# A transformer block with local attention, forward and backward: normalisation in one step, one set of stores on another queue, and a later set of shift copies

## The chip, the core and the metric

The kernel runs on one core of a Trainium2 chip. The core has five engines with instruction streams of their own: TensorE (PE in the profile; PEld is its loading of weights), VectorE (DVE), ScalarE (ACT), GpSimd (POOL) and SyncE (SP). SP computes nothing and issues transfers; ACT and POOL issue transfers as well, between their own instructions. A transfer that an engine issues stands in that engine's instruction stream: it is issued when everything ahead of it in the stream has been and when what it waits for is done. In the profile, SPq, ACTq and POOLq are these issues. The transfers themselves are carried by 16 DMA engines.

The metric is the device time of one execution in microseconds (us), as a median over several executions.

## What is computed

One pre-norm transformer block on x of 2048 rows (S) and 512 columns (D), and the gradients of all its inputs for a given gradient of the output. Everything is bf16.

```python
def _layernorm(x, axis=-1, eps=1e-5):
    m = jnp.mean(x, axis=axis, keepdims=True)
    v = jnp.var(x, axis=axis, keepdims=True)
    return (x - m) / jnp.sqrt(v + eps)

# attention: 32 heads of 16 columns, 8 keys per row at distances 0, 2, ..., 14
idx = pos[:, None] - off[None, :]
logits = jnp.einsum("bhsd,bhswd->bhsw", q, kg) * scale
attn = _softmax(logits, axis=-1)
o = jnp.einsum("bhsw,bhswd->bhsd", attn, vg)

h = x + _A_ref(_layernorm(x, axis=-1), A_wqkv, A_wo)
h2 = h + _B_ref(_layernorm(h, axis=-1), B_w1, B_b1, B_w2, B_b2)   # GELU network, F = 1792

_out, _vjp = jax.vjp(_f, A_x, A_wqkv, A_wo, B_w1, B_b1, B_w2, B_b2)
_grads = _vjp(grad_out)
```

The layernorm has no learned scale or offset. It is applied twice: to x and to h.

## The kernel before

The 2048 rows are worked through in four chunks (NC = 4) of 512 rows (CH), each as four tiles (TPC = 4) of 128 rows, one row per partition. The program has three phases.

Phase 1 (0 to about 185 us) is the forward attention: for each chunk the first layernorm, the projection to q, k and v, the logits, the softmax, the weighted sum over the eight keys, the output projection, h, and the second layernorm. Here a scheduler at build time places the instructions of each engine, by estimated costs, from the program's dependencies. So an edit of one instruction can move others.

Phase 2 (185 to about 380 us) is the GELU network forward and backward, chunk by chunk (p2_h, p2_rest), almost only matmuls. At its end p3_pre works out the gradient of the attention output for chunk 0.

Phase 3 (380 us to the end) is the backward pass of the attention. Its order is written out by hand. The loop `for c in range(NC + 2)` runs over the chunks; within it `slot(us)` is a place where DVE is expected to be busy for so long and PE is filled with other work, which `wgrads` gives out: the matmuls of the weight gradients (ps_gw for the network's weights, ps_gwo and ps_gwq for the attention's). `later(n, cost, fn)` puts a small piece of work (some transposes and a copy, for instance) off by n slots. There is no scheduler behind it: what is called first stands first on its engine.

The pieces that the change touches:

**layernorm (L165 to L180).** For each of the four tiles of a chunk, statistics on DVE: st (L169), then mean and variance into mv (L170), whose last index 0 is the mean and 1 the variance. Then for the four tiles at once: ve, the variance plus epsilon (L173, DVE); rstd, that to the power −1/2 (L174, POOL); nm, which is −mean × rstd (L176, DVE). At last ln for each tile (L178, DVE), x × rstd + nm, with rstd and nm as scalars of each partition. It is called for x (four chunks, ending in ln1) and for h (four chunks, ending in ln2): eight calls, 32 ln instructions. Transposes on PE (pt, L162) read ln.

**to_tm_store (L204 to L219).** It brings a feature-major tile to rows: eight transposes on PE (ptm, L210), one ACT copy of 128x1024 (tmst, L213), one store of 256 KB (L215). It does so twice for a chunk. A further store of 18 KB (L217 or L219) puts the 18 border rows into the neighbour chunk's table. All stores are issued by SP. In phase 1 it writes v_d, k_d and q_d. With `stage` given it is called in p3_pre (L681, chunk 0) and in p3_go (L1054, chunks 1 to 3), and writes go_d, the gradient of the attention output: eight stores of 256 KB and three of 18 KB. POOL then gathers rows of go_d into R (L224). In phase 3 tmst has two buffers.

**What else SP issues in phase 3.** Loads for the weight gradients: gwm (L753, 1 MB, in turn into two buffers, so that a load waits for the matmuls that read the buffer before), ln_r (L741, 1 MB), gqh (L855), and ln1r (L151), vw (L885). ln1r is the chunk's normalised x.

**What ACT does in phase 3.** got (L647, L653), ghT (L163), gqkvT (L280), gqs and gks (L1029), the shift copies sh (L1062), gyr (L184), and gwst (L831): the copy of a finished weight-gradient accumulator (ps_gw, ps_gwo or ps_gwq, pool psF with two buffers) from PSUM, and every second time ACT issues its store. PE can open an accumulator only when gwst has emptied the buffer.

**The products.** R, the rows gathered by POOL, is multiplied on DVE by coefficients cf (prb, L1012; in phase 1 L262). PE sums the products (ps_band, L1026), and ACT copies the sum out.

**shift (L1058 to L1066).** It copies the logit gradients glf (or attn), moved along the rows by 4 × w4, into sh: four ACT copies of 32x1024, one for each quarter of the partitions (about 1 us each). Its `at` gives the number of slots by which each copy is put off. Then `coefs` transposes sh into cf on DVE. For the last chunk (c == NC) the call is

```python
        if c == NC:
            shk = shift(c - 1, glf, (1, 1, 2, 2))
```

and its cf are used by the key part (cfk) four tiles later in that pass; the value part (vtile) is worked on meanwhile.

Of the kernel before, what the change touches and what calls it, by code (L numbers as in the profile page):

```python
# [10 lines left out]
P = 128  # L11
BF16 = mybir.dt.bfloat16
F32 = mybir.dt.float32
ACT = mybir.ActivationFunctionType
ALU = mybir.AluOpType
# [16 lines left out]
def _sub(apobj, dims, off=0):  # L32
    return _ap(apobj, [apobj.ap[0]] + [list(d) for d in dims], off)
# [3 lines left out]
def kernel(  # L37
# [21 lines left out]
    V, A, T, G, SY = nc.vector, nc.scalar, nc.tensor, nc.gpsimd, nc.sync  # L59
# [7 lines left out]
    CH = 512  # L67
    NC = S // CH
    TPC = CH // P
# [33 lines left out]
    def TT(name):  # L103
        return psT.tile([P, 1024], BF16, name=name, tag="t")
# [24 lines left out]
    RPAD = 18  # L129
# [35 lines left out]
    def layernorm(wp, src, rstd_all, c, dst):  # L165
        mv = wp.tile([P, TPC, 2], F32, name="mv", tag="mv", bufs=2)
        for j in range(TPC):
            st = wp.tile([P, 6], F32, name="st6", tag="st6", bufs=2)
            V.bn_stats(out=st[:], in_=src[:, j, :])  # L169
            V.bn_aggr(out=mv[:, j, :], in_=st[:])  # L170
        rs = rstd_all[:, c * TPC:(c + 1) * TPC]
        ve = wp.tile([P, TPC], F32, name="ve", tag="ve", bufs=2)
        V.tensor_scalar(out=ve[:], in0=mv[:, :, 1], scalar1=EPS, scalar2=None, op0=ALU.add)  # L173
        G.tensor_tensor(out=rs, in0=ve[:], in1=mhalf[:], op=ALU.pow)  # L174
        nm = wp.tile([P, TPC], F32, name="nm", tag="nm", bufs=2)
        V.scalar_tensor_tensor(out=nm[:], in0=mv[:, :, 0], scalar=-1.0, in1=rs, op0=ALU.mult, op1=ALU.mult)  # L176
        for j in range(TPC):
            V.tensor_scalar(out=dst[:, j, :], in0=src[:, j, :], scalar1=rs[:, j:j + 1], scalar2=nm[:, j:j + 1],  # L178
                            op0=ALU.mult, op1=ALU.add)

    def ln_bwd_a(wp, ps, rs):
        gyr = wp.tile([P, D], BF16, name="gyr", tag="gyr", bufs=2)
# [19 lines left out]
        ln_bwd_v(wp, gyr, c0, xh, resid, out)  # L202

    def to_tm_store(wp, fm, off, dst, c, back, nb=3, stage=None):  # L204
        for j2 in range(TPC // 2):
            pt = TT("ptm")
            for jj in range(2):
                j = 2 * j2 + jj
                for g in range(4):
                    T.transpose(_sub(pt[:], [[32, DH], [1, 8]], jj * 512 + 8 * g),  # L210
                                fm[:, g, off + j * P:off + (j + 1) * P], Pmat[:])
            st = stage() if stage else wp.tile([P, 2, 512], BF16, name="tmst", tag="tmst", bufs=nb)
            A.copy(out=st[:], in_=pt[:].rearrange("p (a n) -> p a n", a=2))  # L213
            r = j2 * 2 * P + (RPAD if back else 0)
            SY.dma_start(out=dst[c][r:r + 2 * P, :].rearrange("(a p) d -> p a d", p=P), in_=st[:])  # L215
            if back and j2 == 1 and c + 1 < NC:
                SY.dma_start(out=dst[c + 1][0:RPAD, :], in_=st[P - RPAD:P, 1, :])  # L217
            if not back and j2 == 0 and c > 0:
                SY.dma_start(out=dst[c - 1][CH:CH + RPAD, :], in_=st[0:RPAD, 0, :])  # L219

    def gather_rows(R, dst, c, sc, back):
        t = dst[c]
# [303 lines left out]
    glf = glp.tile([P, 2, SP], BF16, name="glf")  # L526
# [128 lines left out]
    def ga_prod(pr, got, vw, g):  # L655
        V.tensor_tensor(out=pr, in0=got[:, g, :].unsqueeze(1).to_broadcast([P, W, 512]),  # L656
                        in1=_sub(vw[:, g, PAD:PAD + 512], [[-DIL, W], [1, 512]]), op=ALU.mult)

    def ga_sum(L, pr, g):
        for hf in range(2):  # L660
            for w4 in range(4):
                T.matmul(L[32 * w4:32 * w4 + 32, hf, :], lhsT=Emat[:, g, :], rhs=pr(2 * w4 + hf),
                         start=(g == 0), stop=(g == 3), skip_group_check=True)
# [141 lines left out]
    def pt3(tag, name=None):  # L805
        if tag in HOME:
            shp, *hs = HOME[tag]
            pl, tg = hs[hpos[tag] % len(hs)]
            hpos[tag] += 1
            return pl.tile(shp, BF16, name=name or tag, tag=tg, bufs=1)  # L810
        shp, nb = P3T[tag]
        return p3.tile(shp, BF16, name=name or tag, tag=tag, bufs=nb)
# [155 lines left out]
    def later(n, cost, fn):  # L968
        pend.append([n, cost, fn])

    def slot(dve_us):
        pe = 0.0
        for x in list(pend):
            x[0] -= 1
            if x[0] <= 0:
                pend.remove(x)
                x[2]()
                pe += x[1]
        filler(dve_us * RATIO - pe)
# [78 lines left out]
    def shift(c, src, at):  # L1058
        sh = pt3("sh")

        def cp(w4):
            A.copy(out=sh[32 * w4:32 * w4 + 32],  # L1062
                   in_=_sub(src[32 * w4:32 * w4 + 32, 0, 0:1], [[SP + 2, 2], [1, 512]], c * CH + 4 * w4))
        for w4 in range(4):
            later(at[w4], 0.0, lambda w4=w4: cp(w4))
        return sh  # L1066
# [33 lines left out]
    for c in range(NC + 2):  # L1100
        if 0 < c < NC:
            got, vw = st3[c]["got"], st3[c]["vw"]
            L = psL.tile([P, 2, 512], F32, name="ps_ga", tag="l")
            for g in range(4):
                pr = pt3("prod", "pr")
                ga_prod(pr[:], got, vw, g)
                later(2, 0.7, lambda pr=pr, g=g, L=L: ga_sum(L, lambda w: pr[:, w, :], g))
                if c >= 2:
                    gln1(c - 2, g)
                slot(2.3 + (1.9 if c >= 2 else 0))  # L1110
            if c + 1 < NC:
                load_vw(c + 1)
        elif c >= NC:
            for g in range(4):
                gln1(c - 2, g)
                slot(2.0)
            if c == NC + 1:
                for _ in range(3):
                    slot(2.0)
                break  # L1120
        if c > 0:
            gt_ = pt3("gqkvT")
            gqkv[c - 1] = gt_
            for sc in range(2):
                later(1 + sc, 1.0, lambda sc=sc, c=c, gt_=gt_: unperm(gqs[c - 1][sc][:], gt_[:, 0:4, :], 4, sc * 256))
            cfv = coefs(pt3, st3[c - 1]["sh"][:, 0, 0:1], 0, 512)

        def vtile(k):
            sc, m = k // 2, k % 2
            if m == 0:  # L1130
                bt["gs"] = pt3("gks")
            gs = bt["gs"]
            band_tile("v", c - 1, sc, m, cfv, gs, 1.0,
                      lambda gs=gs, sc=sc, c=c: unperm(gs[:], gqkv[c - 1][:, 8:12, :], 4, sc * 256))

        if c == NC:
            shk = shift(c - 1, glf, (1, 1, 2, 2))
        if c > 0:
            vtile(0)
            vtile(1)  # L1140
        if 0 < c < NC:
            pp = pt3("pp")
            V.tensor_tensor(out=pp[:], in0=L[:], in1=attn_c(c), op=ALU.mult)
            later(1, 0.9, lambda L=L, pp=pp: ga_rows(L, pp))
        if c > 0:
            vtile(2)
            vtile(3)
        if 0 < c < NC:
            V.tensor_tensor(out=glf[:, :, c * CH:(c + 1) * CH], in0=L[:], in1=attn_c(c), op=ALU.mult)
            if c == 1:  # L1150
                V.memset(glf[:, :, S:SP], 0.0)
        if c < NC:
            cfq = coefs(pt3, glf[:, 0, 0:1], c * CH, SP)
        if 0 < c < NC:
            shk = shift(c - 1, glf, (1, 2, 3, 3))
        if c == NC:
            later(2, 0.0, lambda: open_gates.add("v"))
        if 0 < c < NC - 1:
            p3_go(c + 1)
        if c < NC:  # L1160
            st3[c]["sh"] = shift(c, attn, (4, 5, 6, 7) if c > 0 else (2, 3, 4, 5))
            gqs[c] = []
            for k in range(4):
                sc, m = k // 2, k % 2
                if m == 0:
                    gqs[c].append(pt3("gqs"))
                band_tile("q", c, sc, m, cfq, gqs[c][sc], scale, None)
            if c == NC - 1:
                later(3, 0.0, lambda: open_gates.add("q"))
        if c > 0:  # L1170
            cfk = coefs(pt3, shk[:, 0, 0:1], 0, 512)
            for k in range(4):
                sc, m = k // 2, k % 2
                if m == 0:
                    bt["gs"] = pt3("gks")
                gs = bt["gs"]
                band_tile("k", c - 1, sc, m, cfk, gs, scale,
                          lambda gs=gs, sc=sc, c=c: unperm(gs[:], gqkv[c - 1][:, 4:8, :], 4, sc * 256))
            if c == NC:
                slot(0.5)  # L1180
                slot(0.5)
                slot(0.5)
                open_gates.add("k")
# [53 lines left out]
```

## Time and profile before

| | us |
|---|---|
| median of 4 executions | 663.56 |
| the four | 665.61, 661.72, 660.21, 665.4 |
| the profiled execution | 670.66 |
| its span (first to last instruction) | 668.5 |

The page of the profile gives busy time by engine, the span in 40 slices and the chain of work that ended last. Two lines of the slices:

```profile
PEclk9899999898889999999999999999999999999999
DMA  9483848744999996997995999886798679997621
```

Each digit is a slice of 16.7 us. PEclk is the TensorE clock granted, in tenths of full speed (9 is 90% or more); DMA is the mean busy share of the 16 DMA engines. Two lines of the waits of SP's queue tell what its stream stood still for: in total, how often, and the longest time.

```profile
SPq L215 <- ACT tmst L213: 162.7, 26, 24.0
SPq L753 <- PE ps_gw L896: 51.9, 6, 14.3
```

In an engine's timeline a line has the start, the duration, the engine, the code line, the operation with its tiles and shapes, the number of instructions, and in brackets the idle time before it with what ended it. In a chain a line has start, duration and the work, in order of time.

### The profile page before, as it was taken

Reading aid. Unit: us, or ns where it says so; the run is one execution under the profiler, and the core shown is the slowest. Engines: PE = TensorE matmul, PEld = TensorE weight load, DVE = VectorE, ACT = ScalarE, POOL = GpSimd, SP = SyncE. Lnnn points to the kernel's source line nnn. Section 1 sums busy time; section 2 is a strip of 40 time slices with the busy share of each in tenths; the row PEclk is TensorE's granted clock in tenths of the full one; section 3 lists DMA queues with packets and bytes.
Section 4 is the critical chain, followed back from the end, with each engine's and each line's share of the span. In section 5 each row is a group of like instructions: output and inputs, shape, how many; then the busy total and the mean of one; then the engine's idle time right before and its main releaser. Section 6 shows DMA issues by size and latency. Waiting matters only on the chain.

```text
span 668.5 us, 10227 instructions
## 1 busy us (share of the span) xinstructions
PE 600.9 (90%) x3916; PEld 289.7 (43%) x3916; DVE 517.7 (77%) x760; ACT 375.7 (56%) x601; POOL 150.0 (22%) x183
## 2 busy tenths in 40 slices
PE   3889989696699989999999979989999999979897
PEld 1343444342344434444444433434466667434343
DVE  7889979878889768888849769867877789569230
ACT  2497878688585457377351353673368337455321
POOL 3341536431101110110110222221232023112010
PEclk9899999898889999999999999999999999999999
DMA  9483848744999996997995999886798679997621
GB/s 288 158 268 127 293 154 293 237 144 94 225 245 208 233 248 139 248 235 159 258 289 156 277 333 370 305 292 249 236 392 288 255 232 332 363 306 254 206 79 47
DMA packets 147947, 158.98 MB, mean 238 GB/s; under 512 B 94476, under 2 KB 132540, under 8 KB 141244
## 3 DMA queue, kind: packets, MB, share of 16 engines
q1 hardware_dynamic: 120076, 69.58, 41.1%
q0 software_dynamic: 15376, 77.63, 33.5%
q10 hardware_dynamic: 12448, 11.14, 5.2%
q8 instruction: 30, 0.49, 0.3%
q14 instruction: 17, 0.14, 0.1%
HBM read 87.76 MB, written 48.03 MB: 203 GB/s over the span
## 4 chain that ended last, share of the span: by engine, by line
PE 59%; ACT 11%; DMA 9%; DVE 6%; issue 5%; POOL 2%; SPq 0%; ACTq 0%; DVEq 0%; POOLq 0%
PE ps_gg L622 7%; PE ps_gl L1082 6%; PE ps_gl L636 6%; PE ps_gwq L924 6%; PE ps_gw L904 6%; PE ps_gw L896 5%; PE ps_h L577 4%; PE ps_f L610 4%; DMA gwm<-gT_d 3%; PE ps_band L1026 2%; PE ps_gwo L914 2%; PE ptu L279 2%; DMA R<-k_d,rowi 2%; DMA goT<-in_grad_out_dram 2%; ACT sh L1062 1%
## 5 line engine op out<-in xcount | busy, mean ns | idle before, releaser
L1012 DVE TENSOR_TENSOR prb<-R,cf 128x2048 bf16<-128x2048 bf16 x96 | 111.5, 1219 | 29.8 <-PE ps_band L1026 22.8
L184 ACT ACTIVATE gyr<-ps_gl,rstd 128x512 bf16<-128x512 f32 x32 | 22.0, 687 | 86.1 <-PE ps_gl L636 48.8
L577 PE MATMUL ps_h<-ln2T,w 128*128 128x512 bf16 x224 | 58.3, 390 | 4.4 <-ACT xa L579 4.0
L896 PE MATMUL ps_gw<-gout_r,gwm 128*128 128x512 bf16 x224 | 53.1, 384 | 3.3 <-DMA gwm<-gT_d 3.3
L622 PE MATMUL ps_gg<-goT,w2T 128*128 128x512 bf16 x224 | 54.5, 379 | 0.9 <-DVE gb1p L624 0.8
L610 PE MATMUL ps_f<-w,gt 128*128 128x512 bf16 x224 | 51.3, 379 | 3.9 <-ACT h2s L613 2.0
L904 PE MATMUL ps_gw<-gwm,ln_r 128*128 128x256 bf16 x448 | 52.9, 273 | 0.7 <-ACT gwst L831 0.7
L636 PE MATMUL ps_gl<-w1T,dt 128*128 128x512 bf16 x224 | 52.0, 379 | 0.6 <-ACT gyr L184 0.4
L924 PE MATMUL ps_gwq<-gqh,ln_r 128*128 128x512 bf16 x192 | 44.9, 386 | 6.0 <-ACT gwst L831 3.7
L341 PE MATMUL ps_qkv<-ln1T,wqkv 128*128 128x512 bf16 x192 | 48.0, 393 | 0.7 <-DMA go_d<-zrow 0.6
L656 DVE TENSOR_TENSOR pr<-got,vw 128x4096 bf16<-128x4096 bf16 x16 | 36.2, 2286 | 14.9 <-ACT got L653 9.8
L904 PEld LDWEIGHTS <-ln_r 128*128 128x128 bf16 x448 | 43.0, 98 | 9.2 <-issue 3.0
L578 ACT ACTIVATE xb<-ps_h,b1c 128x512 bf16<-128x512 f32 x56 | 38.3, 693 | 12.5 <-DVE xa L589 6.5
L624 DVE CUSTOM_DVE_ANT_0 dt<-ps_gg,dt 128x512 bf16<-128x512 f32 x56 | 37.6, 684 | 8.2 <-PE ps_gg L622 8.1
L579 ACT ACTIVATE xa<-ps_h,b1c 128x512 bf16<-128x512 f32 x56 | 38.3, 699 | 7.4 <-DVE dt L590 7.4
L562 POOL DMA_DIRECT2D gT_d<-tst x16 | 12.0, 750 | 134.2 <-DMA tst<-gt 132.1
L280 ACT COPY gqkvT<-ptu 128x1024 bf16<-128x1024 bf16 x24 | 24.3, 1011 | 31.3 <-PE ptu L279 31.2
L262 DVE TENSOR_TENSOR prb<-R,cf 128x2048 bf16<-128x2048 bf16 x32 | 37.6, 1210 | 3.8 <-DMA R<-v_d,rowi 2.8
L232 DVE TENSOR_TENSOR pr<-qt,kt 128x4096 bf16<-128x4096 bf16 x16 | 36.1, 2284 | 2.1 <-PE ps_band L267 1.1
L213 ACT COPY tmst<-ptm 128x1024 bf16<-128x1024 bf16 x32 | 31.3, 1022 | 7.3 <-PE ptm L210 4.6
L610 PEld LDWEIGHTS <-gt 128*128 128x128 bf16 x224 | 21.6, 98 | 31.4 <-DVE gt L585 3.4
L577 PEld LDWEIGHTS <-w 128*128 128x128 bf16 x224 | 22.0, 100 | 28.7 <-issue 6.6
(182 smaller groups left out, 1133.8 us busy)
## 6 DMA issues: line engine op xcount, KB each, us to landing
gwm<-ghT_d SPq DMA_DIRECT2D x7, 1024.0 KB, 4.9
gT_d<-tst POOLq DMA_DIRECT2D x12, 512.0 KB, 5.0
ghT_d<-tst POOLq DMA_DIRECT2D x12, 512.0 KB, 5.4
gwm<-gT_d SPq DMA_DIRECT2D x6, 1024.0 KB
out_dram<-gwst ACTq DMA_DIRECT2D x22, 256.0 KB, 9.8
ln_d<-ln POOLq DMA_DIRECT2D x8, 512.0 KB, 4.6
vw<-vf_d SPq DMA_DIRECT2D x4, 528.0 KB
xt<-in_A_x_dram SPq DMA_DIRECT2D x4, 512.0 KB, 9.2
```

Source lines behind the costliest of these rows:

```text
L341: T.matmul(ps[:], lhsT=wqkv[:, dc, sel * D + g * P:sel * D + (g + 1) * P], rhs=st_[c]["ln1T"][:, dc, :], start=(dc == 0), stop=(dc == DC - 1))
L577: T.matmul(ps[:], lhsT=wcol(w1, dc, f), rhs=ln2T[c][:, dc, :], start=(dc == 0), stop=(dc == DC - 1))
L578: A.activation(out=xb[:, f - f0, :], in_=ps[:], func=ACT.Identity, bias=b1c[:, f:f + 1])
L579: A.activation(out=x2[:, f - f0, :], in_=ps[:], func=ACT.Square, bias=b1c[:, f:f + 1])
L610: T.matmul(ps[:], lhsT=gts[f // 4][:, f % 4, j * P:(j + 1) * P], rhs=wrow(w2, f), start=(f == 0), stop=False)
L622: T.matmul(ps[:], lhsT=wcol(w2T, dc, f), rhs=goT[:, dc, :], start=(dc == 0), stop=(dc == DC - 1))
L636: T.matmul(ps[:], lhsT=dts[f // 4][:, f % 4, j * P:(j + 1) * P], rhs=wrow(w1T, f), start=(f == 0), stop=(f == FT - 1))
L896: yield from mm_pair("ps_gw2", lambda ps, o, u, i, t, k: T.matmul(ps[:], lhsT=g_[:, o, i * HN + t, :], rhs=gout_r[i][:, t, :], **k), MM, w ...
L904: yield from mm_pair("ps_gw1", lambda ps, o, u, i, t, k: T.matmul(ps[:, 256 * u:256 * u + 256].rearrange("p (a f) -> p a f", a=2), lhsT=ln ...
L924: yield from mm_pair("ps_gwq", lambda ps, o, u, i, t, k: T.matmul(ps[:], lhsT=ln1_r[i][:, t, (2 * d2 + o) * P:(2 * d2 + o + 1) * P], rhs=h ...
L1012: V.tensor_tensor(out=pr[:, 4 * hf:4 * hf + 4].rearrange("p j (d h) -> p j d h", h=H), in0=R[:, o:o + 4, :].rearrange("p j (d h) -> p j d ...
L1082: T.matmul(ps[:], lhsT=gqkv[c][:, b, j * P:(j + 1) * P], rhs=wqkvT[b // 4][:, b % 4, :], start=(b == 0), stop=(b == 11))
```

## The change

Three edits. First, nm is no longer computed, and ln is (x − mean) × rstd: the same DVE instruction with subtraction and multiplication in place of multiplication and addition, and with the mean in mv and rstd as its scalars. Second, to_tm_store issues its stores on ACT's queue where `stage` is given, which is for go_d; the stores of phase 1 stay with SP. Third, the last shift's copies are put off by 1, 2, 3 and 3 slots in place of 1, 1, 2 and 2.

```diff
@@ layernorm
         G.tensor_tensor(out=rs, in0=ve[:], in1=mhalf[:], op=ALU.pow)
-        nm = wp.tile([P, TPC], F32, name="nm", tag="nm", bufs=2)
-        V.scalar_tensor_tensor(out=nm[:], in0=mv[:, :, 0], scalar=-1.0, in1=rs, op0=ALU.mult, op1=ALU.mult)
         for j in range(TPC):
-            V.tensor_scalar(out=dst[:, j, :], in0=src[:, j, :], scalar1=rs[:, j:j + 1], scalar2=nm[:, j:j + 1],
-                            op0=ALU.mult, op1=ALU.add)
+            V.tensor_scalar(out=dst[:, j, :], in0=src[:, j, :], scalar1=mv[:, j, 0:1], scalar2=rs[:, j:j + 1],
+                            op0=ALU.subtract, op1=ALU.mult)
@@ to_tm_store
     def to_tm_store(wp, fm, off, dst, c, back, nb=3, stage=None):
+        Q = A if stage else SY
...
-            SY.dma_start(out=dst[c][r:r + 2 * P, :].rearrange("(a p) d -> p a d", p=P), in_=st[:])
+            Q.dma_start(out=dst[c][r:r + 2 * P, :].rearrange("(a p) d -> p a d", p=P), in_=st[:])
             if back and j2 == 1 and c + 1 < NC:
-                SY.dma_start(out=dst[c + 1][0:RPAD, :], in_=st[P - RPAD:P, 1, :])
+                Q.dma_start(out=dst[c + 1][0:RPAD, :], in_=st[P - RPAD:P, 1, :])
             if not back and j2 == 0 and c > 0:
-                SY.dma_start(out=dst[c - 1][CH:CH + RPAD, :], in_=st[0:RPAD, 0, :])
+                Q.dma_start(out=dst[c - 1][CH:CH + RPAD, :], in_=st[0:RPAD, 0, :])
@@ the loop of phase 3
         if c == NC:
-            shk = shift(c - 1, glf, (1, 1, 2, 2))
+            shk = shift(c - 1, glf, (1, 2, 3, 3))
```

In the changed order SP's stream differs only by the eleven stores. On ACT each store stands directly behind the copy of its data: copy, store, border store, copy, store. On PE, DVE and POOL the order of phases 2 and 3 is the same as before. In phase 1 the scheduler also moves a few other instructions on the engines; on DVE the four ln instructions of h now stand directly behind the wait for rstd. In the last pass of phase 3, one sh copy instead of two stands ahead of two gwst copies, and the three others stand behind the next gqkvT copy, ahead of gks.

## The prediction

> **What bounds the kernel now.** I read the page's busy times and slices first, then the chain of waits, then engine timelines and four-microsecond windows at each edited place.
>
> ```profile
> PE 600.9 (90%) x3916; PEld 289.7 (43%) x3916; DVE 517.7 (77%) x760; ACT 375.7 (56%) x601; POOL 150.0 (22%) x183
> PE 59%; ACT 11%; DMA 9%; DVE 6%; issue 5%; POOL 2%; SPq 0%; ACTq 0%; DVEq 0%; POOLq 0%
> ```
>
> TensorE (PE) carries the time. The edits touch VectorE (DVE), ScalarE (ACT) and SyncE (SP), so each counts only where PE or the chain waits for it. PE's busy share by stage (windows): 89% in 10–100 us, 78% in 100–185, 97% in 185–380, 90% in 380–480, 97% in 480–560, 90% in 560–668. The layernorms lie before 185, the moved stores at 353–509, the last shift copies at 598. Three pieces of the chain matter:
>
> ```profile
> 370.38 8.40 PE ps_gl L636 x39
> 378.78 11.23 DMA R<-k_d,rowi
> 390.03 3.40 DVE prb L1012 x3
> ...
> 437.89 0.99 ACT gqs L1029 x2
> 438.88 0.91 ACT tmst L213
> 441.37 8.21 DMA gwm<-gT_d
> 449.62 1.04 PE ps_gw L896 x4
> ...
> 597.44 0.99 ACT gqkvT L280
> 598.43 0.94 ACT sh L1062
> 599.38 1.04 ACT sh L1062
> 600.45 0.59 ACT gwst L831
> 601.09 1.01 PE ps_gwq L924 x2
> ```
>
> First: a gather of 11.23 us ends the start of phase 3. Second: a gwm load leaves only after a tmst copy of ScalarE. Third: PE's accumulator is freed by a gwst copy that stands behind two sh copies. PE's own timeline gives the prices of the last two in its brackets:
>
> ```profile
> 449.62 1.04 PE L896 MATMUL ps_gw<-gout_r,gwm 128*128 128x512 bf16 x4 [2.29 <-DMA gwm<-gT_d]
> 601.09 1.01 PE L924 MATMUL ps_gwq<-gqh,ln_r 128*128 128x512 bf16 x2 [3.73 <-ACT gwst L831]
> ```
>
> **Layernorm.** Removed: eight nm instructions, 144 to 266 ns each (1.3 us of DVE). Before seven of them DVE stood idle 6.0 us together, until POOL's rstd:
>
> ```profile
> L176 DVE SCALAR_TENSOR_TENSOR nm<-mv,rstd x8: 144/162/266, 8.7 to 168.2; 128x4 f32<-128x4 f32 x8
>   POOL rstd L174: 6.0, 7
> ```
>
> That wait does not go: the ln instructions need rstd too and inherit it. So the sure part is a nm (0.16 us) per layernorm, and what the scheduler makes of it. In the changed order the four ln stand directly behind the rstd wait, where before one 1.2 us prb multiplication stood between nm and ln. So ln of the second projection's first chunk starts at 84.88 instead of 86.09, and of the second at 114.28 instead of 115.49. The third (nm 140.25, ln 140.45) and fourth (168.23) win 0.2 to 0.5 us. Against it, a softmax step that had run in the gap moves behind the ln (113.25 to about 115.6). The ln starts of the four chunks come 1.2, 1.2, 0.2 and 0.5 us sooner; PE is 78 to 89% busy here and has other chunks' work meanwhile, so I take a third of these 3.1 us: −1.0 us. Bounds: −3 (the gather behind the third prb, for which DVE waits 2.78 us until 130.63, leaves 2 us sooner, and 1 us more at the other chunks) and +2 (that softmax step 2.3 us late, mostly on the path).
>
> The new form (subtract, then multiply, scalars mean and rstd) is not in the trace. Nearest rows: the present ln (multiply, add, same shape) at 0.406 us and L194 at 0.41; from the other side the single-pass statistics of the same 128x512 (L169) at 0.68. I take 0.41, since only the two operators differ from L178. At 0.68 it is 32 × 0.27 = 8.6 us of DVE, a third to all of it on the path: +2.9 to +8.6.
>
> The Trainium skill ("VectorE: DVE Perf Modes", "The perf-mode tier table") gives the tensor-scalar form of bf16 in SBUF its fastest mode by source and type and lists no exception for an operator; by it the slow bound is excluded and this term stays −1.0.
>
> **Stores on ScalarE's queue.** Eleven DMAs (eight of 256 KB, three of 18 KB) leave SP and are issued by ScalarE, directly behind the copy that fills them. Their data and landing stay; only who waits differs. SP stood 162.7 us, 26 times, behind tmst copies, the largest sum of its queue, but this matters only where something urgent is next. Chunk by chunk:
>
> Chunk 0 (353.84): next on SP is a transpose gated by a DVE result (357.43), and ScalarE is idle from 354.7 to 372.1. Zero.
>
> Chunk 1 (stores 390.47 to 391.68): behind them is a 1 MB load of ln_r (392.26), not needed before about 480. Freed, it can leave at about 383. It then shares the DMA engines with the 11.23 us gather that is on the chain; the windows from 380 to 392 show them 92 to 99% busy at 311 to 392 GB/s. A full megabyte ahead is 1/0.37 = 2.8 us. So 0 to +2.8; I take +1, since more than half of the gather's 11.23 us is over when the load could start to count.
>
> Chunk 2 is the second piece of the chain:
>
> ```profile
> 439.81 0.37 SPq L215 DMA_DIRECT2D go_d<-tmst  x1
> 440.23 0.42 SPq L219 DMA_DIRECT2D go_d<-tmst  x1
> 440.76 0.51 SPq L215 DMA_DIRECT2D go_d<-tmst  x1
> 441.37 6.32 SPq L753 DMA_DIRECT2D gwm<-gT_d  x2
> ```
>
> The gwm load needs its buffer, whose last reader on PE ends at about 439.2. Without the stores it leaves 2.1 us sooner and PE waits 0.2 instead of 2.29: −2.1, bounds −2.3 and 0 (the engines are 92 to 100% busy from 440 to 452, so the load may leave sooner and land when it did). Next late is DVE's prb, which waited 3.87 us for PE and moves with it.
>
> Chunk 3 (507.70): the following gwm load waits for PE until 510.74. Zero.
>
> ScalarE pays about 0.42 us per issue (442.28, 0.38; next instruction at 442.70), 1.3 us in each of chunks 1 to 3. Behind it at chunk 1: sh 391.25 and gqs 393.37, needed later. At chunk 2: sh 440.73, then gwst at 441.68 becomes 443.2; PE needs that accumulator at about 443.7. At chunk 3 likewise 513.1 against 514.2. So +0.2, bounds 0 and +1.0. The second store of each chunk leaves about 0.9 us later than from SP, and POOL's gather of these rows (396.21, 444.07, 511.27) with it; at the first the gathered rows are wanted at 410.35, some 3 us after landing, and at the second not before 471. Zero, with +0.9 as bound. Waits for the rotating DMA semaphores add nothing: every transfer eight places earlier lands well before.
>
> The Trainium skill ("DMA: Bandwidth & Descriptors", "Issuing engines are not separate DMA queues") speaks against this edit: all issuers share the same 16 engines and another issuer saves only sequencer time. By that rule alone chunk 2 gives 0 instead of −2.1 and the sum below is 2.1 higher; the row of 441.37 shows a load held by another's data, which the rule does not price.
>
> **Last shift.** One sh copy (1.0 us) instead of two now stands before gwst of 600.45, the rest one slot on. PE's 3.73 us wait becomes 2.7. The moved copies are done by about 606.1, and the transposing step that reads them feeds prb no sooner than 609. The later wait (gqh load behind prb of 619.49, 5.20 us, PE waits 2.32) moves with PE; the end is PE (ps_gwq, 15.45 us). −1.0, bounds −1.1 and 0.
>
> **Cold clock.** After both PE waits the granted clock falls: 0.73 in 452–456, 0.62 in 600–604. There a band group took 1.69 us instead of 0.98 and eleven matmuls 3.40 instead of 2.38 (1.7 us in all); after 601.09, eight transposes took 0.85 instead of 0.45 and eleven matmuls 3.14 instead of 2.40 (1.1). Shorter waits may spare some: −2.8 to 0. I take 0 for both, as 2.7 us remain idle at 601 and other idle places show a drop too.
>
> **Sum.** −1.0 + 1.0 − 2.1 + 0.2 − 1.0 = −2.9. The profiled execution took 670.66 us (span 668.5, 2.2 us around it) and becomes 667.8. It was 7.1 above the median of 663.56, so the median becomes 660.7.
>
> **Rivals.**
> (a) Further gain: the clock stays up at 449 and 601 (−2.8) and the layernorm shifts reach PE (−3 instead of −1), with the gather of 378.78 undisturbed (−1): −8.7, 655. For it: PE idles 22% of 100–185. Against: three favours at once. 0.18.
> (b) The change does not do what it says: the gwm load lands as before (DMA engines full) and PE's gain at 601 is taken back at the load of 620.52. Then −1 + 1 + 0.2 = 0, 663.8. Against: that load waits for PE's own band result. 0.15.
> (c) Slower: the new ln form takes 0.68 us. Place: DVE before 185, busy 84 to 91%. With all of it on the path −2.9 + 8.6 = +5.7, 669.3; with a third, 663.6. It decides from 0.09 us more per ln (32 × 0.09 = 2.9). For it: no row of this form. 0.10.
> (d) Slower: ScalarE becomes late. Its 1.3 us per chunk reaches PE at chunks 1 to 3 (ScalarE is on the chain for most of 427–441): +3.9, with the full +2.8 of ln_r and no gain at chunk 2: −1 + 2.8 + 3.9 − 1.0 = +4.7, 668.3. It decides once gwst is over 0.5 us late at 443.7. 0.15.
> My forecast's own case has 0.42, range 657 to 663.
>
> **Chances.** A measurement of this kernel tells about 1% (6.6 us) from no change. Faster by over 1% comes from (a), 0.15 of its 0.18, and 0.06 of the own case; slower from (c) with ln_r's full +2.8 (+7.5) and from (d) with the layernorm's +2 (+7.7), 0.08 each. Rest 0.63. The range runs from 655 (a) to 668.3 (d): outside are those parts of (c) and (d) as far as they pass it, 0.12, and the far end of (a), 0.06.
>
> **What would show it.** The ln rows at 0.41 us; ln_r issued near 383 and the first gather's length against 11.23; gwm issued near 439.3 and PE's wait below 1 us at 449; PE's wait near 2.7 us at 600; gwst not later than PE. An ln row at 0.68, a first gather over 13 us, or a new PE wait for gwst in 440–450 would prove the forecast wrong.

## The result

The changed kernel takes 0.9954 of the time before, with a 95% interval of 0.9932 to 0.9977: 3 us less (1.5 to 4.5), where the forecast had 2.9 us less. The medians of all executions are 665.79 us (42) against 667.58 (63). The ratio, like those below, compares the executions within about 1.5% of the fastest of their kernel; all executions together give 0.9973 by their medians and 0.9987 by their means. The single executions scatter far more than the gain, from 656.8 to 679.5 us, so a single profile is no measure of the whole time, and the argument below rests on stages of many profiles.

The two profiled executions show the scatter: 670.66 us before, 661.70 after, a difference of 9.0, of which two thirds are chance if the ratio is right. The profile after, first its busy times and the head of its chain:

```profile
PE 600.1 (91%) x3916; PEld 288.2 (44%) x3916; DVE 516.1 (78%) x752; ACT 376.7 (57%) x601; POOL 152.0 (23%) x183
PE 6%; DVE 2%; DMA 1%; ACT 0%; issue 0%; DVEq 0%
```

PE's busy time is the same. The chain could only be followed back to 597 us here, so its shares say nothing; its last part does:

```profile
607.28 2.36 DVE prb L1011 x2
609.65 0.02 issue
609.66 5.62 DMA gqh<-gv_d
615.28 0.04 issue
615.32 2.56 PE ps_gwq L923 x8
617.88 1.86 PE ps_band L1025 x16
```

It runs through DVE and a load, where before it ran through PE from 601 to 619. PE's timeline at the two edited places, and at the later load, first the lines of the kernel before that the prediction does not show:

```profile
442.41 4.92 PE L896 MATMUL ps_gw<-gout_r,gwm 128*128 128x512 bf16 x22
...
450.59 1.76 PE L1026 MATMUL ps_band<-prb,S 128*32 128x512 bf16 x16
452.29 3.47 PE L896 MATMUL ps_gw<-gout_r,gwm 128*128 128x512 bf16 x11
...
625.76 1.89 PE L924 MATMUL ps_gwq<-gqh,ln_r 128*128 128x512 bf16 x8 [2.32 <-DMA gqh<-gv_d]
```

and of the changed kernel:

```profile
436.55 6.00 PE L895 MATMUL ps_gw<-gout_r,gwm 128*128 128x512 bf16 x26
442.48 1.05 PE L1025 MATMUL ps_band<-prb,S 128*32 128x512 bf16 x16
443.46 2.55 PE L895 MATMUL ps_gw<-gout_r,gwm 128*128 128x512 bf16 x11
...
589.87 0.59 PE L923 MATMUL ps_gwq<-gqh,ln_r 128*128 128x512 bf16 x2 [2.54 <-ACT gwst L830]
...
609.91 1.25 PE L923 MATMUL ps_gwq<-gqh,ln_r 128*128 128x512 bf16 x5 [1.46 <-DMA gqh<-gv_d]
615.32 2.56 PE L923 MATMUL ps_gwq<-gqh,ln_r 128*128 128x512 bf16 x8 [3.07 <-DMA gqh<-gv_d]
```

Three readings. The wait of 2.29 us for the gwm load has no bracket any more, and the band group after it takes 1.05 in place of 1.76: the granted clock is 1.00 from 436 to 456 us, where before it was 0.73 from 452 to 456. The wait for gwst is 2.54 in place of 3.73. But the load of gqh, for which PE waited 2.32 us before, now stops it twice, for 4.53 us, and the granted clock is 0.57 from 616 to 620.

The cause of the first is seen in SP's and ACT's timelines of the changed kernel:

```profile
433.51 8.53 SPq L752 DMA_DIRECT2D gwm<-gT_d  x2
```

```profile
432.90 1.03 ACT L212 COPY tmst<-ptm 128x1024 bf16<-128x1024 bf16 x1
433.96 0.37 ACTq L214 DMA_DIRECT2D go_d<-tmst  x1
434.65 0.31 ACTq L218 DMA_DIRECT2D go_d<-tmst  x1
435.05 1.01 ACT L212 COPY tmst<-ptm 128x1024 bf16<-128x1024 bf16 x1 [1.11 <-issue]
436.09 0.37 ACTq L214 DMA_DIRECT2D go_d<-tmst  x1
```

The load left at 433.51, while the first tmst copy was still running. The run of ps_gw matmuls at 436.55 began at 442.41 in the profile before, 5.86 us later; the load left there at 441.37, 7.86 us later. Within the pass it is 2.0 us sooner, as the forecast had it. The layernorm's rows (instruction, times, ns at least, median, at most):

```profile
L176 DVE TENSOR_SCALAR ln<-xt,mv,rstd x16: 395/408/527, 8.6 to 41.3; 128x512 bf16<-128x512 bf16 x16
L176 DVE TENSOR_SCALAR ln<-h,mv,rstd x16: 394/406/539, 82.6 to 167.4; 128x512 bf16<-128x512 bf16 x16
```

The new form costs what the old one did (0.406 us).

### The profile page after: what moved, and what is told of

The parts are those of the page before. It is cut to its first block, busy times and chain, and to the rows that moved or that the text cites. A ratio compares the mean times of both kernels' runs of the same rounds, so it can differ in the third digit from the quotient of the medians.

```text
span 659.5 us, 10221 instructions
## 1 busy us (share of the span) xinstructions
PE 600.1 (91%) x3916; PEld 288.2 (44%) x3916; DVE 516.1 (78%) x752; ACT 376.7 (57%) x601; POOL 152.0 (23%) x183
## 5 line engine op out<-in xcount | busy, mean ns | idle before, releaser
L279 ACT COPY gqkvT<-ptu 128x1024 bf16<-128x1024 bf16 x24 | 24.3, 1011 | 27.0 <-PE ptu L278 26.9
L212 ACT COPY tmst<-ptm 128x1024 bf16<-128x1024 bf16 x32 | 31.4, 1016 | 8.0 <-PE ptm L209 3.8
L609 PEld LDWEIGHTS <-gt 128*128 128x128 bf16 x224 | 21.8, 99 | 31.1 <-issue 3.4
L635 PEld LDWEIGHTS <-dt 128*128 128x128 bf16 x224 | 21.4, 98 | 29.1 <-DVE gb1p L623 2.4
```

Source lines behind the costliest of these rows:

```text
L609: T.matmul(ps[:], lhsT=gts[f // 4][:, f % 4, j * P:(j + 1) * P], rhs=wrow(w2, f), start=(f == 0), stop=False)
L635: T.matmul(ps[:], lhsT=dts[f // 4][:, f % 4, j * P:(j + 1) * P], rhs=wrow(w1T, f), start=(f == 0), stop=(f == FT - 1))
```

## The experiments

The executions of one kernel differ by some us in phases 1 and 2 (the FFN phase took 162.3 to 172.1 us in profiles of kernels with the same instructions there). So each profile was read by stages, from starts of instructions that every kernel has: phase 1 to the first h2s copy; the second pass from the 7th to the 11th gwst copy of ps_gw; the last stage from the 28th of these to the last gwst of all. Phase 1 is counted from the start of the span, each other stage is a difference of two starts in ACT's timeline, all in us.

| kernel | ratio (95%) | phase 1 | second pass | last stage |
|---|---|---|---|---|
| before | 1 | 186.3 | 30.8 | 96.8 |
| changed | 0.9954 (0.9932 to 0.9977) | 182.1 | 26.9 | 97.6 |
| e1_ln | 1.0041 (0.9998 to 1.0084) | 183.9 | 31.0 | 96.1 |
| e2_stores | 0.9944 (0.9908 to 0.9981) | 185.5 | 27.1 | 98.7 |
| e3_shift | 1.0023 (0.9983 to 1.0064) | 182.7 | 29.4 | 96.6 |
| e4_noshift | 0.9960 (0.9907 to 1.0012) | 183.9 | 26.9 | 96.3 |
| e5_gqh_r8 | 0.9990 (0.9951 to 1.0028) | 184.5 | 26.9 | 97.7 |
| e7_oldln | 0.9987 (0.9945 to 1.0029) | 183.5 | 27.1 | 98.0 |
| e8_c23 | 0.9950 (0.9903 to 0.9996) | 184.7 | 27.0 | 96.5 |
| e9_c01 | 1.0010 (0.9968 to 1.0051) | 184.5 | 31.1 | 96.2 |
| e10_vstore | 0.9972 (0.9925 to 1.0018) | 181.9 | 26.9 | 99.1 |
| e11_vstore_noshift | 0.9953 (0.9919 to 0.9988) | 181.2 | 26.9 | 96.7 |
| e12_byhalf | 0.9916 (0.9878 to 0.9954) | 184.2 | 26.9 | 92.4 |
| e13_half | 0.9915 (0.9885 to 0.9944) | 185.2 | 26.9 | 100.7 |
| e14_half_noshift | 0.9899 (0.9860 to 0.9938) | 181.6 | 26.9 | 93.0 |
| e15_before_half | 0.9965 (0.9937 to 0.9993) | 184.0 | 31.4 | 94.4 |
| e16_oldln_half | 0.9944 (0.9906 to 0.9983) | 184.7 | 27.1 | 92.9 |
| e17_newln_half | 0.9960 (0.9919 to 1.0001) | 181.6 | 26.9 | 93.8 |

The profiled execution of e13_half lost 7.7 us ahead of the last ps_gwo copy: from the 28th gwst copy to there it took 39.3 us, the others 31.5 to 33.0. Its last stage would be about 93.0 without this.

**Each edit alone, and the change without the shift.** The edits are those of the diff, one at a time on the kernel before (e1, e2, e3), and for e4 on the changed kernel:

```diff
-            shk = shift(c - 1, glf, (1, 2, 3, 3))
+            shk = shift(c - 1, glf, (1, 1, 2, 2))
```

e1, the layernorm:

> Only the layernorm edit. Theory 1 (the gain comes from the stores; the layernorm is a small help, the shift is given back): -1 us, ratio 0.998 to 1.000. Theory 2 (the forecast's split, layernorm -1.0, stores -0.9, shift -1.0): -1 us as well. Theory 3 (the new order of phase 1 makes the gain; in the two traces the last matmul of the first attention is 3.7 us earlier): -3 us, ratio 0.9955, with phase 2 beginning 3 to 4 us sooner than in this call's unchanged kernel.

e2, the stores:

> Only the stores on ScalarE's queue. Theory 1: PE's wait for the gwm load at the second pass (2.29 us before) gone, the clock kept there, the 1.04 us wait for the gwm load of the first pass gone: -3 to -4.5 us, ratio 0.993 to 0.9955. Theory 2: -0.9 us, ratio 0.9986, with the first gather lengthened by about 1 us over 11.2. Theory 3: 0, ratio 1.000.

e3, the shift:

> Only the last shift on slots 1, 2, 3, 3. Theory 1: PE's wait for gwst at the third last piece falls from 3.7 to about 2.6 us and its clock stays up, but the gqh load behind DVE's products leaves no sooner, so that PE's wait for gqh grows from 2.3 to 4 or 5 us: total 0 to +0.9 us, ratio 1.000 to 1.0015. Theory 2: -1.0 us, ratio 0.9985, with the wait for gqh still 2.3 us.

e4, all but the shift:

> The changed kernel with the last shift back on slots 1, 1, 2, 2. Theory 1: as fast as the changed kernel or up to 0.9 us faster, ratio 0.994 to 0.9955 against the kernel before. Theory 2: 1.0 us slower than the changed kernel, ratio 0.997.

The stores alone give 0.9944, the whole gain; no gain of either of the other two shows by itself. Theory 3 (phase 1 makes it) falls with e1, and theory 2, the forecast's split, with e2 and with e3's trace: PE's wait for gwst is 2.54 us there, but the one for gqh 3.25 and not 2.3, and the last stage is no shorter (96.6 against 96.8). Theory 1 had the clock stay up at gwst in e3; it was 0.57 from 598 to 602. e4's interval is too wide to tell theories 1 and 2 apart.

**Which stores.** On the kernel with the stores alone, the choice of the queue is narrowed:

```diff
-        Q = A if stage else SY
+        Q = A if stage and c >= 2 else SY     # e8
+        Q = A if stage and c < 2 else SY      # e9
```

> The kernel before with only the stores of chunks 2 and 3 on ScalarE's queue. Theory 1: the whole gain of the stores is at the gwm load of the second pass: that stage 4.1 us shorter, first gather and first pass as before, ratio 0.993 to 0.9945. The forecast: -2.1 us, ratio 0.997.

> The kernel before with only the stores of chunks 0 and 1 on ScalarE's queue; ln_r leaves near 378 us then. The forecast: first gather about 1 us longer, ratio 1.0015. Theory 1: the gather is lengthened by 0.3 us at most and nothing else moves, ratio 1.000. Theory 6 (the slower stretch at 385 to 415 us in two of the three runs with these stores, 24.1 us against 21.5, comes from them): that stretch 24 us again, ratio 1.004.

Chunks 2 and 3 alone give 0.9950; chunks 0 and 1 alone 1.0010. PE's timeline at the second pass in e9, where chunk 2's stores are with SP:

```profile
450.89 1.04 PE L897 MATMUL ps_gw<-gout_r,gwm 128*128 128x512 bf16 x4 [2.55 <-DMA gwm<-gT_d]
451.86 1.71 PE L1027 MATMUL ps_band<-prb,S 128*32 128x512 bf16 x16
453.50 3.52 PE L897 MATMUL ps_gw<-gout_r,gwm 128*128 128x512 bf16 x11
```

and in e8, where they are not:

```profile
438.02 6.05 PE L897 MATMUL ps_gw<-gout_r,gwm 128*128 128x512 bf16 x25
444.00 1.05 PE L1027 MATMUL ps_band<-prb,S 128*32 128x512 bf16 x16
444.98 2.55 PE L897 MATMUL ps_gw<-gout_r,gwm 128*128 128x512 bf16 x11
```

The wait is one part, the slow matmuls after it the other: 1.71 against 1.05 and 3.52 against 2.55, with a granted clock of 0.57 from 452 to 456 us in e9 and of 1.00 from 440 to 448 in e8. The second pass takes 27.0 us in the thirteen kernels with chunk 2 on ScalarE (26.9 to 27.1) and 30.7 in the five without (29.4 to 31.4): 3.8 us. Chunk 3's stores lie in the stretch behind it, from the 11th to the 28th gwst copy, which takes 110.8 us in all eighteen profiles, so they give nothing and the 3.8 us are kept.

e3 separates the two parts. Its load is late like the others', but the clock was 1.00 from 449 to 453:

```profile
449.37 1.04 PE L896 MATMUL ps_gw<-gout_r,gwm 128*128 128x512 bf16 x4 [2.46 <-DMA gwm<-gT_d]
450.33 1.05 PE L1026 MATMUL ps_band<-prb,S 128*32 128x512 bf16 x16
451.31 2.55 PE L896 MATMUL ps_gw<-gout_r,gwm 128*128 128x512 bf16 x11
```

Its pass takes 29.4 us, 2.4 more than without the wait; in the four others, where the clock fell (0.57 to 0.68 over the 4 us behind the wait), it takes 30.8 to 31.4. So the wait costs 2.4 us, and the fall of the clock 1.5 to 2.0 more where it comes.

The ln_r load left 3 to 4 us after the first gather's issue in the thirteen kernels with chunk 1 on ScalarE, and 12 to 14 us after it in the five others. From that issue to DVE's first product it took 11.0 us in the mean of the former (10.1 to 11.5) and 10.7 of the latter (9.5 to 11.3). So a cost of the early load does not show: 0.3 us in the mean, well inside the spread. Theory 6 is not settled: from p3_pre's first tmst copy to the 5th gwst copy the former took 61.6 to 68.3 us, mean 65.1, the latter 63.9 to 66.4, mean 64.6. PE's wait for the gwm load of the first pass varies there in both groups; in e2, whose theory 1 had it gone, it was 2.09 us, in the kernel before 1.04, and in the changed kernel it is gone.

**The layernorm.** e7 is the changed kernel with the old layernorm:

> The kernel before with the stores and the shift, so the changed kernel with the old layernorm. Theory 2 (layernorm edit gains 1 us): ratio 0.997. Theory 5 (the new order of phase 1 costs something, as the run with the layernorm edit alone had 1.004): 2 us faster than the changed kernel, ratio 0.992. Theory 1: within 1 us of the changed kernel, ratio 0.994 to 0.996.

e16 and e17 differ in the layernorm alone and ran on one chip; both have the stores, the old shift and the half-by-half edit shown below.

> The kernel before with the stores on ScalarE's queue and the value part's first pair half by half; old layernorm, old shift. If the layernorm edit is worth the 1.0 us of the forecast (the traces so far: the first row output of the network is 1.3 us earlier with the new form, on average of seven and seven profiles): 1 us slower than the same kernel with the new layernorm, ratio 0.992, with that first output at 184.6 us. If it costs (the run with the layernorm alone: 1.004): 2 us faster, ratio 0.987.

> The same with the new layernorm, on the same chip beside it: ratio 0.990 as in its first run, and its first row output of the network at 183.3 us.

The first h2s copy starts at 183.0 us in the mean of ten profiles with the new form and at 184.5 of eight with the old: 1.5 us sooner, with a standard error of 0.6. The timed runs do not agree on it: 0.9944 with the old form and 0.9960 with the new, 1.0041 for the edit alone, but 0.9987 for the changed kernel with the old form (e7) against 0.9954. Theory 5, a gain of 2 us from the old form (0.992), falls with e7. The intervals are too wide for 1 us (0.15%). What the layernorm edit is worth stays open.

**Where the shift's gain went.** First the rows buffer: the second gqh load of the value part gets a buffer that nothing else holds.

```diff
-            t_ = pt3("rows", "gqh")[:, 0:HN, :]
+            t_ = pt3("rows", "gqh")[:, 0:HN, :] if i == 0 else rtile("gqh", 2)
```

> The changed kernel, with the second gqh load of the value part in the buffer of 8 KB that the attention weight gradient has left free, in place of a buffer of the gathered rows. Theory 1 (what the shift wins at 590 us is taken back because this load waits for DVE's products to leave a rows buffer): the load leaves several us before 609.7, PE's two waits for gqh (1.46 and 3.07 us) shrink to 1.5 or less together, 3 us less than the changed kernel, ratio 0.991. Theory 4 (the load waits for the store of the value gradient's last rows): it leaves when it did, waits and time as in the changed kernel, ratio 0.995.

Theory 1 falls as it was put. The load left 19.5 us after the first ps_gwq matmul (19.8 in the changed kernel), and its chain shows what it waits for:

```profile
607.62 7.72 DMA gv_d<-gks
...
615.46 5.84 DMA gqh<-gv_d
621.30 0.04 issue
621.35 3.00 PE ps_gwq L923 x8
```

The store of the last value rows takes 7.72 us to land, and the load follows it. In the changed kernel both ends lie together: the store, issued at 601.55, landed 7.9 us later, and DVE's products left the rows buffer at 609.64. So they do in the kernel before, where the store, issued at 614.37, landed at 620.35 and the product of 619.49 ended at 620.53; the store stands in the waits of SP's queue there:

```profile
SPq L855 <- DMA gv_d<-gks: 10.4, 1, 10.4
```

Next, that store was put on ScalarE's queue, right behind its own copies, with the shift (e10) and without (e11):

```diff
-                G.dma_start(out=g3_d[sel][:, 4 * c + 2 * sc:4 * c + 2 * sc + 2, :], in_=gs[:])
+                (A if kind == "v" and c == NC - 1 and sc == 1 else G).dma_start(out=g3_d[sel][:, 4 * c + 2 * sc:4 * c + 2 * sc + 2, :], in_=gs[:])
```

> The changed kernel with the second gqh load of the value part in the free buffer and, besides, the last store of the value gradient (gv_d from gks) issued by ScalarE behind its own copies, not by GpSimd. Theory 4 (the load waits for this store, which took 7.9 us to land): the store lands sooner, the load leaves before 15 us after the first ps_gwq matmul (19.5 before), PE's waits for gqh fall from 4.5 us to 2 or less, and the clock stays up there: 2 to 4 us less than the changed kernel, ratio 0.987 to 0.992. Rival (both gates are lifted and the DMA engines are the limit): waits stay at 4 us, ratio 0.995.

> The same with the last shift on its old slots. Theory 4: with the later wait gone the shift's gain at the weight-gradient copy (1.15 us, and up to 1.6 of clock) is no longer taken back, so this one is 1 to 2.8 us slower than the run with the shift. Rival (the shift gains nothing in any case): the same time.

The chain of e10:

```profile
602.46 7.22 DMA gv_d<-gks
...
609.83 6.35 DMA gqh<-gv_d
616.17 0.04 issue
616.22 2.92 PE ps_gwq L923 x8
```

The store takes 7.22 us to land from ScalarE too, the load leaves no sooner (20.5 us after the first ps_gwq matmul), and the wait stays at 4.42 us, so e11 could not show what it was made for. What it shows is that the last stage is 2.4 us longer with the shift than without (99.1 against 96.7).

The twelve profiles of kernels without the half-by-half order (below) show why. PE goes on behind the load 57.1 to 58.5 us after the 28th gwst copy in the five with the shift and 57.1 to 58.0 in the seven without: PE's earlier start does not bring this moment forward. What then differs is the clock behind the wait. In seven kernels (before, e1, e3, e4, e8, e9, e11) it was 1.00 over the next 4 us, and the last stage took 96.1 to 96.8 us; in five (changed, e2, e5, e7, e10) it was 0.57 to 0.63, and the stage took 97.6 to 99.1. The waits before it were 1.89 to 3.25 us in the former and 3.07 to 4.42 in the latter. PE's lines in e2, without the shift:

```profile
596.28 0.59 PE L925 MATMUL ps_gwq<-gqh,ln_r 128*128 128x512 bf16 x2 [3.72 <-ACT gwst L832]
...
621.41 3.46 PE L925 MATMUL ps_gwq<-gqh,ln_r 128*128 128x512 bf16 x8 [4.13 <-DMA gqh<-gv_d]
```

At last the wait was covered rather than shortened: the value part's first two accumulators take the first half of the rows both, and only then the second half, so that PE has eight more matmuls before it needs the late load.

```diff
-                    wg_sink(wrows(out_2, 2 * d2 * P, 2, sel * D, D)), by_half=(si == 0 and d2 == 0))
+                    wg_sink(wrows(out_2, 2 * d2 * P, 2, sel * D, D)), by_half=(si <= 1 and d2 == 0))
```

e12 has it on top of e10, e13 on the changed kernel, e14 on e4, e15 on the kernel before.

> The run with the moved value store, and the value part's first pair of accumulators worked half by half, so that the second gqh half is wanted 8 matmuls (1.7 us) later. Theory 4: what is left of the wait for gqh falls by up to 1.7 us; the two accumulators close together, which may cost 0.6 us at the next pair: 0 to 1.5 us less than the run without it.

> The changed kernel with the value part's first pair of accumulators worked half by half and nothing else. Theory 4 (what the shift wins is taken back at the load that follows the last value store): PE has 8 more matmuls to do before it needs that load, the second wait (3.07 us) falls to 1 us or less and the clock stays up: 3 to 5 us less than the changed kernel, ratio 0.988 to 0.992.

> The same with the last shift on its old slots. Theory 4: the shift's 1.15 us at the gwst copy is now kept, so this one is 1.0 to 2.8 us slower than the run with the shift from the last ps_gw copy to the end. Rival (another wait takes the shift's gain back): the same length of that stage.

> The kernel before with the value part's first pair of accumulators half by half only. There the wait for the load was 2.3 us: 1.5 to 3 us less than the kernel before, ratio 0.9955 to 0.998, by theory 4; no change if something else is behind it by as much.

The later wait is gone, and the last stage is 92.4 to 94.4 us. PE's timeline in e12 at the first load, the only wait for a load left there:

```profile
612.23 1.25 PE L923 MATMUL ps_gwq<-gqh,ln_r 128*128 128x512 bf16 x5 [0.91 <-DMA gqh<-gv_d]
```

and in e14:

```profile
597.94 0.59 PE L923 MATMUL ps_gwq<-gqh,ln_r 128*128 128x512 bf16 x2 [3.73 <-ACT gwst L830]
...
616.88 1.25 PE L923 MATMUL ps_gwq<-gqh,ln_r 128*128 128x512 bf16 x5 [0.36 <-DMA gqh<-gv_d]
```

With the shift PE is 1.2 us earlier and then waits 0.55 us longer for the first load; in e13, which differs from e14 in the shift alone, it is 1.43 against 0.36. That load takes back half to nearly all, and e13 is not faster than e14 (ratios 0.9915 and 0.9899, last stages of about 93.0 and 93.0). So the rival of e14's expectation holds too: covering the second load does not free the gain, for the first is as late. The half-by-half edit itself is worth 2.4 us on the kernel before, by its profile (96.8 to 94.4) and by its ratio (0.35% of 664 is 2.3). Together with the stores it gives 0.990 to 0.996 in its five runs, the three fastest versions here among them; against the changed kernel's 0.9954 that is probably a gain, but every interval overlaps that kernel's own.

## Why the prediction was right or wrong

The sum came out, −2.9 against −3.0: on the 663.56 us that it started from the ratio gives 660.5, against 660.7 and a range of 657 to 663 (timed beside the changed kernel, the kernel before took 667.58 itself). That is luck. Three terms behind the sum were off by about 1 us or more, not all in one direction: the stores gave 3.8 us and not 2.1, the shift gave nothing where 1.0 was counted, and the 1.0 charged for the ln_r load does not show. By the means of the stages the pass gives −3.8 and the last stage, with the shift, +1.0; what phase 1 adds stays open, so the measured 3.0 us are not split to the last microsecond. That the likeliest case was a move of less than 1% holds, but its reason, that a measurement of this kernel tells no less than about 1% from no change, failed: the interval here is 0.23% to either side, and the gain is clear of it.

**The cold clock, "I take 0 for both".** This is the step that mis-sized the gain. The mechanism at chunk 2 was right: the gwm load leaves 2.0 us sooner and the wait of 2.29 us is gone. But where the wait goes, the fall of the clock goes with it, 1.7 us by the forecast's own rows and 1.5 to 2.0 by the passes with and without it (e3). The pass is 3.8 us shorter in the mean, not 2.1, and e8 and e9 show that it is these stores. The argument for 0 ("2.7 us remain idle at 601") was about the other place; at 449 nothing remained idle.

**The last shift, "the later wait … moves with PE".** This step was false. PE's wait at gwst fell by 1.19 us, a little more than the forecast said. But the first gqh load of the value part left 41.3 to 41.6 us after the 28th gwst copy in all kernels but the disturbed e13, with the shift or without, and the second 51.2 to 52.6 us after it. The forecast's chain named the product of 619.49 alone as what this load waits for; the store had landed only 0.2 us before that product ended. The second load is set by DVE's products and by this store, which takes 6 to 8 us to land, and PE's earlier start only makes it wait longer. In e3 the last stage is as long as before; in the kernels without the half-by-half edit it is 97.8 us in the mean of five with the shift and 96.8 of seven without. The edit is worth nothing, and costs where the longer wait brings the clock down behind it (97.6 to 99.1 us against 96.1 to 96.8). e2 shows the same without the shift. There the clock stayed up at 596 us, PE came early to the load, waited 4.13 us, and the eight matmuls behind it took 3.46 us (1.89 before), so the stage grew to 98.7. Rival (b) had this half right: it named the load of 620.52 as the place where PE's gain is taken back, and was argued away with "that load waits for PE's own band result".

**The ln_r load, +1.** The load left earlier than thought, at 377.94 in the changed kernel, before most of the gather had run, and from the gather's issue to DVE's first product the kernels with the early load took 0.3 us more in the mean, inside the spread of 10.1 to 11.5. Although the DMA engines were busy at 92 to 99%, one more megabyte did not delay the gather by its own length (2.8 us); the bound of 0 was the right end.

**ScalarE's issues, +0.2.** Right in kind: from the 7th to the 9th gwst copy it took 18.4 us in the profile before and 20.0 with the stores, so the copy comes 1.6 us later, close to the 1.5 of the forecast, and no wait of PE for it shows (the longest wait of PE in that pass is 0.55 us in the changed kernel, for got, as before). Rival (d) needed PE to be stopped by it and falls with that.

**The layernorm, −1.0.** Rival (c) falls: the new form takes 0.406 to 0.408 us. The term itself is supported by phase 1 in the profiles (1.5 ± 0.6 us, a standard error) and not by the timed runs; it stays open. The "VectorE: DVE Perf Modes" page of the Trainium skill ("The perf-mode tier table") prices the tensor-scalar form by source and type and lists no exception for an operator; the rows agree for this pair of operators, both at 0.41 us.

**The rule against the stores.** The page "DMA: Bandwidth & Descriptors" of the Trainium skill ("Issuing engines are not separate DMA queues") would have given this part 0. The measurement decides: the edit gave 3.8 us. What was saved was more than the issue time, about 0.4 us each: the load, its buffer already free, stood behind stores that waited for ScalarE's copies, and the fall of the clock behind PE's wait went with that wait.

## What to carry to other kernels

A transfer that waits for another engine's data holds up everything behind it on its issuing queue; put it on the queue of the engine that makes the data, and count the gain with the fall of the clock that the ended wait may have brought. Before pricing a shorter wait of the busiest engine, find what sets its next wait: if that is a chain on another engine (here products, copy, store, load), the gain is only carried there and lost. Cover such a wait with work that does not need the late data, as the half-by-half order did.

## What the runs showed of the hardware

The length of PE's wait alone did not decide whether the granted clock fell. At the gwm load of the second pass, waits of 2.29 to 2.87 us brought it down in four kernels of five (0.57 to 0.68 over the next 4 us), and one of 2.46 (e3) did not. At the second gqh load, waits of 1.89 to 2.68 us left it at 1.00 in six of six, and waits of 3.07 to 4.42 brought it down in five of six. After the same wait of 3.73 us at gwst it fell in eight profiles without the shift and not in three (e2, e14, e16): from the last ps_gwo copy to the first of ps_gwq it took 9.7 to 10.1 us in the former and 8.42 in the latter, the matmuls between being the same. After the 2.54 us with the shift it fell in two of seven (e3, e10). What else decides is not shown.

The last value store of 256 KB took 5.9 to 7.9 us to land, whether GpSimd (5.9 in e17, 6.0 in the kernel before, 7.9 in the changed one) or ScalarE (7.22 in e10) issued it; the stretch from 600 to 608 us of the changed kernel had the DMA engines busy at 97 to 99%.

The middle of phase 3, from the 11th to the 28th gwst copy, took 110.8 us in all eighteen profiles (110.78 to 110.84), while the FFN phase (from the first h2s copy to p3_pre's first tmst copy) varied by 10 us with the same instructions. Chance sits in a few stretches; a comparison by stages sees effects that the whole time hides.
